# The arctangent's table booked by itself, and a one-column Gelu before the gate's tanh, in an S4D and channel-MLP kernel

## The chip, the cores and the metric

The kernel runs on one core of one Trainium2 chip. The metric is the device time of one execution in microseconds (us); the times before are three runs of the same program. The five engines have queues of their own, which run in order: TensorE (PE, with its weight loads as PEld), VectorE (DVE), ScalarE (ACT), GpSimd (POOL) and SyncE (SP, which only issues DMAs here).

## What is computed

One sequence of L = 2048 tokens with D = 576 channels goes through two branches, whose product is added to the input:

```python
x  = A_u
xn = _layernorm(x)
s  = _A_ref(xn, ...)          # S4D: a kernel K of L taps per channel, then a causal convolution by FFT
g  = _silu(_B_ref(xn, ...))   # layernorm, 576 -> 4608, tanh-Gelu, 4608 -> 576
return x + s * g
```

In `_A_ref` the taps come from 128 complex poles for each channel, `K = 2 Re sum_n C exp(A dt l)`. Everything is float32.

## The kernel before

**The MLP sets the frame.** Weights and activations are split into a high and a low float32r part, so each product is three matmuls. The 4608 hidden columns are taken in 12 groups of 384 (`G = 3` blocks of 128), the tokens in two halves of 1024, and each half in two blocks of 512: 48 slots in all, `NSLOT`. A slot has 11 positions on PE. The first three are `layer1` (L508, 14 matmuls of 512 columns each): a PSUM bank is filled, ScalarE applies Gelu (L541) and copies the high part (L544), VectorE forms the low part `hl` (L547). Gelu writes into a tile `h32` of which there are two, and which comes free when `hl` has been formed. The other eight positions are `layer2` (L565, matmuls of 288 columns), whose sums VectorE adds to `acc` (L573). Each group's weights are split on ScalarE (L488) and VectorE (L485).

**S4D fills the gaps.** `params()` turns the pole parameters into polar form once, on 128 x 576 tiles. Its ScalarE steps are Exp, Square, Sqrt, then Arctan (L709), Abs (L710) and Sin (L711, L714). The powers (Exp, L741) are made in eight packs of two halves each; `columns` (L744 to L746) puts phases and weights into a pack, which L753 sends to DRAM. From there 36 blocks of tables are built, each with two Sin on ScalarE (L802, L804) between Copy, Abs and VectorE's products; TensorE makes the taps from them (L867, copied out in L872), VectorE's `skip` (L951) adds the skip weight to the first tap, and the FFT work of a chunk of 96 channels takes the taps in (L939, L977, L1030, L1057).

**The gate.** When a half's last group has been added to `acc`, in the middle of the kernel, `gate_store` forms SiLU of the first half's sums as `z (1 + tanh(z/2))`: two halves of each of 8 tiles, so 16 Tanh of 288 columns (L578, `tanh_half`), each followed by a product on VectorE (L589). Tanh's results go into the same two `h32` tiles as Gelu's. At the same place the transposed second half of the tokens is loaded, transposed on VectorE (L1234) and split (L1239, L1241 on ScalarE, L1246, L1248 on VectorE).

**The order is planned while the program is traced.** The class `Order` keeps a clock for each engine, `od.t`, advances it by booked durations (`act(n) = 0.06 + 0.00098 n` us on ScalarE, for instance), and pins every engine's instructions in the order in which it picked them. It also keeps `od.tbl`, the function table that it thinks ScalarE holds. A step names its table in `tbl` ("gelu", "exp", "sqrt", "sin", "silu"); a step without one leaves the table as it is. A step of another table is booked 1.28 us later (`take`, L87 to L94):

```python
if tbl and tbl != self.tbl:
    free += 1.28
    self.tbl = tbl
```

A step that can wait is admitted only if it ends before the next deadline on its engine, with the load for it and the load back to Gelu counted (`advance`, L167 to L171):

```python
after = st["tbl"] or self.tbl
d += 1.28 * ((after != self.tbl) + (after not in ("gelu", "silu")))
if b > horizon or b + d > soon.get(e, 1e9) + st["late"]:
    continue
```

`soon` holds the latest start of the next Gelu. Among steps that could start, the earliest goes first, and at equal times the line that stands earlier in the list of lines: the weight split before the powers. The planner only orders: the loads themselves are put in by the compiler, in front of an activation whose function is not in the table loaded last. Instructions added inside a step's function, without a step of their own, are not booked.

Of the kernel before, what the change touches and what calls it, by code (L numbers as in the profile page):

```python
# [12 lines left out]
AF = mybir.ActivationFunctionType  # L13
# [29 lines left out]
def dve(n):  # L43
    return 0.075 + 0.00104 * n


def act(n):
    return 0.06 + 0.00098 * n
# [159 lines left out]
def step(eng, dur, fn, need=(), mark=None, cv=0, at=0.0, late=0.0, tbl=None, by=1e9):  # L208
    return dict(eng=eng, dur=dur, fn=fn, need=tuple(need), mark=mark, cv=cv, at=at, late=late, tbl=tbl, by=by)
# [3 lines left out]
def mixer_kernel(ctx, tc, u, log_a_real, a_imag, c_real, c_imag, log_dt, d_skip, w1, b1, w2, b2,  # L213
                 f1, f2, g2, g1, tvals, ident, out, parts=("mlp", "s4d")):
    nc = tc.nc
# [40 lines left out]
    tv, small = tvs[:, :NV], tvs[:, NV:]  # L256
    b1t = sb.tile([P, F // P], F32, name="b1t")
    halfpi, epst = small[:, 0:2], small[:, 2:4]
# [316 lines left out]

    def tanh_half(z):
        t = sb.tile([P, TB], F32, name="h32", bufs=2)[:, :288]
        nc.scalar.activation(t, z, AF.Tanh, scale=0.5)  # L578
        return t

    def gate_store(j, dh):
        z = acc[:, j, dh * 288:dh * 288 + 288]
        T = []

        def one():
            T.append(tanh_half(z))

        def two():
            nc.vector.scalar_tensor_tensor(z, T[0], 1.0, z, op0=OP.add, op1=OP.mult)  # L589
            if dh:  # L590
                nc.gpsimd.dma_start(g_s[j], acc[:, j])
        return one, two
# [71 lines left out]
    def params():  # L664
# [4 lines left out]
        add = lambda *a, **k: out.append(step(*a, **k))  # L669
# [14 lines left out]
        V, A = nc.vector, nc.scalar  # L684
        e, d = act(D) + 0.1, dve(D)
# [15 lines left out]
        t = T[2]  # L701
# [4 lines left out]
            add("DVE", 1.9, lambda h=h: V.reciprocal(t[:, h], t[:, h]))  # L706
        add("DVE", d, lambda: V.scalar_tensor_tensor(ci, T[4], 1.0, ci, op0=OP.subtract, op1=OP.mult))
        add("DVE", d, lambda: V.tensor_mul(t, t, ci))
        add("ACT", e, lambda: A.activation(t, t, AF.Arctan), tbl="sin", late=0.0)  # L709
        add("ACT", e, lambda: A.activation(T[3], t, AF.Abs))  # L710
        add("ACT", e, lambda: A.activation(T[3], T[3], AF.Sin, bias=halfpi[:, 0:1], scale=-2.0), tbl="sin", late=0.0)  # L711
        turns(1, th)
# [379 lines left out]
    od = Order(tc, nc)  # L1092
# [234 lines left out]
    for x, y in zip((pl, pl2, pl3, pl4, pl5, pl6), params()):  # L1327
        x["steps"] += y
# [103 lines left out]
    for slot in range(NSLOT):  # L1432
# [4 lines left out]
        for pos in range(NPOS):  # L1437
# [21 lines left out]
            else:  # L1459
# [12 lines left out]
                if last or halves:  # L1472
                    add = cell[0]
# [76 lines left out]
```

## Time and profile before

| What | us |
|---|---|
| median of 3 runs (lowest to highest) | 1084.84 (1084.74 to 1085.39) |
| the profiled execution, its time | 1084.85 |
| the profiled execution, its span | 1083.1 |
| PE busy in the span | 1072.6 (99%) |
| DVE busy | 947.7 (88%) |
| ACT busy | 653.0 (60%) |
| POOL busy | 199.4 (18%) |
| mean granted TensorE clock | 0.998 |

The span runs from the first to the last recorded instruction; 1.75 us of the execution's time lie outside it. Times in rows of the timeline are microseconds from the span's start, then the duration, the engine, the source line, the operation, the tile written and the tiles read; a bracket at the end of a row holds the idle time of the engine before it, and what ended it. Matmuls overlap, so a TensorE row is longer than the distance to the next one.

### The profile page before, as it was taken

How to read it: one execution, taken by the hardware profiler on the slowest of the kernel's cores; microseconds unless marked ns; L12 is line 12 of the kernel's file. 1: busy time of each engine (PE TensorE's matmuls, PEld its weight loads, DVE VectorE, ACT ScalarE, POOL GpSimd, SP SyncE). 2: the span in 40 equal slices, each digit the busy share in tenths (PEclk: the TensorE clock that was granted, in tenths of full speed). 3: DMA queues.
4: the chain of work that ended last, by engine and by line, in shares of the span. 5: the costliest groups of instructions: out<-in, count | busy, mean ns of one | idle time of the engine just before them, and what ended most of it. 6: DMA issues, size and time to landing. Idle time of an engine off the chain costs nothing.

```text
span 1083.1 us, 27198 instructions
## 1 busy us (share of the span) xinstructions
PE 1072.6 (99%) x11491; PEld 933.4 (86%) x11491; DVE 947.7 (88%) x1518; ACT 653.0 (60%) x974; POOL 199.4 (18%) x281
## 2 busy tenths in 40 slices
PE   9999999999999999999999999999999999999997
PEld 7989999889888888888888888888888887888896
DVE  7797878989999999999999999999999996677367
ACT  6558569767666665767756667566665754233333
POOL 6559342110000200002000010000100022110231
PEclk9999999999999999999999999999999999999999
DMA  7746455823225222454423432142312347332344
GB/s 235 231 138 191 152 196 192 215 85 116 71 70 108 67 80 58 108 94 128 134 68 99 83 85 83 37 124 47 107 53 76 111 88 238 111 105 88 96 153 117
DMA packets 136537, 125.54 MB, mean 116 GB/s; under 512 B 88156, under 2 KB 108096, under 8 KB 135392
## 3 DMA queue, kind: packets, MB, share of 16 engines
q1 hardware_dynamic: 120624, 76.44, 26.4%
q0 software_dynamic: 15040, 46.40, 13.7%
q8 instruction: 90, 1.47, 0.6%
q10 hardware_dynamic: 752, 0.97, 0.3%
q14 instruction: 31, 0.25, 0.1%
HBM read 95.52 MB, written 34.01 MB: 120 GB/s over the span
## 4 chain that ended last, share of the span: by engine, by line
PE 87%; DVE 3%; ACT 1%; issue 1%; DMA 1%; POOL 0%; ACTq 0%; DVEq 0%; POOLq 0%
PE mxa L565 19%; PE mxb L565 19%; PE mxa L508 19%; PE mxb L508 19%; PE cv L977 3%; PE cv L867 3%; PE cv L1030 2%; PE cv L939 2%; PE cv L1057 1%; DMA xn_s<-w 0%; DVE hl L547 0%; ACT L541 0%; DVE acc L573 0%; DVE A L644 0%; ACT A L741 0%
## 5 line engine op out<-in xcount | busy, mean ns | idle before, releaser
L565 PE MATMUL mxa<-w2h,hh 128*128 128x288 f32 x573 | 171.4, 299 | 0.0
L565 PE MATMUL mxb<-w2h,hh 128*128 128x288 f32 x576 | 170.9, 297 | 0.0
L565 PE MATMUL mxb<-w2h,hl 128*128 128x288 f32 x576 | 170.1, 295 | 0.2 <-DVE hl L547 0.2
L565 PE MATMUL mxb<-w2l,hh 128*128 128x288 f32 x576 | 169.5, 294 | 0.0
L565 PE MATMUL mxa<-w2h,hl 128*128 128x288 f32 x573 | 169.1, 295 | 0.0
L565 PE MATMUL mxa<-w2l,hh 128*128 128x288 f32 x573 | 168.7, 294 | 0.0
L547 DVE TENSOR_TENSOR hl<-h,hh 128x512 fp32r<-128x512 f32 x144 | 99.4, 692 | 76.3 <-ACT hh L544 75.7
L541 ACT ACTIVATE h<-mxa,b1t 128x512 f32<-128x512 f32 x73 | 50.2, 689 | 126.5 <-PE mxa L508 121.8
L767 POOL DMA_DIRECT2D par<-par_s x36 | 27.3, 759 | 518.9 <-DVE mg L810 479.1
L565 PEld LDWEIGHTS mxa<-w2h,hh 128*128 128x128 f32 x573 | 107.6, 188 | 9.6 <-issue 6.0
L565 PEld LDWEIGHTS mxb<-w2h,hh 128*128 128x128 f32 x576 | 108.2, 188 | 4.9 <-issue 2.5
L565 PEld LDWEIGHTS mxb<-w2l,hh 128*128 128x128 f32 x576 | 108.1, 188 | 0.6
L565 PEld LDWEIGHTS mxb<-w2h,hl 128*128 128x128 f32 x576 | 108.1, 188 | 0.4 <-DVE hl L547 0.4
L565 PEld LDWEIGHTS mxa<-w2l,hh 128*128 128x128 f32 x573 | 107.6, 188 | 0.7
L565 PEld LDWEIGHTS mxa<-w2h,hl 128*128 128x128 f32 x573 | 107.5, 188 | 0.0
L541 ACT ACTIVATE h<-mxb,b1t 128x512 f32<-128x512 f32 x71 | 48.9, 689 | 75.9 <-PE mxb L508 73.7
L544 ACT ACTIVATE hh<-h 128x512 fp32r<-128x512 f32 x144 | 90.9, 632 | 4.0
L573 DVE TENSOR_TENSOR acc<-mxa,acc 128x576 f32<-128x576 f32 x88 | 65.4, 743 | 17.0 <-PE mxa L565 16.7
L508 PE MATMUL mxa<-XH,w1h 128*128 128x512 f32 x284 | 80.3, 404 | 0.0
L508 PE MATMUL mxb<-XH,w1h 128*128 128x512 f32 x280 | 77.3, 398 | 0.2 <-ACT h L541 0.2
L508 PE MATMUL mxa<-XL,w1h 128*128 128x512 f32 x284 | 76.2, 390 | 0.0
L508 PE MATMUL mxa<-XH,w1l 128*128 128x512 f32 x284 | 76.0, 389 | 0.0
(230 smaller groups left out, 2422.3 us busy)
## 6 DMA issues: line engine op xcount, KB each, us to landing
raw<-in_B_w_dram SPq DMA_DIRECT2D x72, 288.0 KB, 3.5
raw<-in_B_w_dram SPq DMA_DIRECT2D x96, 192.0 KB, 3.0
par_s<-A POOLq DMA_DIRECT2D x8, 1080.0 KB, 5.9
par<-par_s POOLq DMA_DIRECT2D x36, 240.0 KB, 3.4
f2t<-f2q SPq DMA_DIRECT2D x24, 256.0 KB, 3.7
raw<-in_B_w_dram SPq DMA_DIRECT2D x48, 96.0 KB, 3.5
u_s<-in_A_u_dram POOLq DMA_DIRECT2D x16, 288.0 KB, 4.4
xc<-xn_s SPq DMA_DIRECT2D x48, 96.0 KB, 3.9
```

What stands on the lines that cost most here:

```text
L508: nc.tensor.matmul(q, a, b, start=j == 0, stop=j == len(ops) - 1)
L541: nc.scalar.activation(t, q, AF.Gelu_apprx_tanh, bias=b1t[:, g * G + i:g * G + i + 1], scale=1.0)
L544: LAST[0] = nc.scalar.activation(hh[:, i], t, AF.Copy)
L547: nc.vector.tensor_sub(hl[:, i], t, hh[:, i].bitcast(F32))
L565: nc.tensor.matmul(q[:, dh, :288], a[:, i, c], b[:, i, d], start=i == 0 and k == 0, stop=i == G - 1 and k == 2)
L573: nc.vector.tensor_add(o, q[:, dh:dh + n, :288], b if g == 0 else o)
L767: nc.gpsimd.dma_start(PAR[b].rearrange("p (g i) k -> p g (i k)", g=4), dram(par_s, (b // 6 * CH + b % 6 * 4) * NPAR, [[D * NPAR, P], [24 * ...
L867: nc.tensor.matmul(q[32 * g:32 * g + 32, i // 2, i % 2 * 64:i % 2 * 64 + 64], U[:, ri, 4 * g + i, :], v[:, ri, 4 * g + i, :], start=ri == ...
L939: nc.tensor.matmul(Q1ST[i, x][g // 2][64 * f:64 * f + 64, g % 2].rearrange(order), f1t[r].rearrange("p s k -> p (s k)"), rhs(r, f), start= ...
L977: nc.tensor.matmul(Q[i][32 * q:32 * q + 32, f, 2 * ri:2 * ri + 2], m[r, 4 * i + q, 32 * ri:32 * ri + 32], A2[r, 4 * p + 2 * i + q // 2, :, ...
L1030: nc.tensor.matmul(QI[q // 2][64 * f:64 * f + 64, q % 2, i], MAT["g2t", p + i // 2][r, i % 2, ri], YS[p + i // 2][0][r, i % 2, ri, f], sta ...
L1057: nc.tensor.matmul(Q[f][32 * e:32 * e + 32, t], g1t[r], A2[r, k:k + 2, 1].rearrange("p i d r -> p i r d"), start=True, stop=True, skip_gro ...
```

## The change

Two edits. The step of the arctangent names a table of its own, "arctan", where it had named "sin". And `tanh_half` applies Gelu to one column, into a spare column of the tile of small constants, in front of Tanh, when the planner's `od.tbl` is not "gelu" at that moment; the planner books nothing for it, and nothing reads the column. What is computed is the same.

```diff
     def tanh_half(z):
         t = sb.tile([P, TB], F32, name="h32", bufs=2)[:, :288]
+        if od.tbl != "gelu":
+            nc.scalar.activation(small[:, 5:6], epst[:, 0:1], AF.Gelu_apprx_tanh)
         nc.scalar.activation(t, z, AF.Tanh, scale=0.5)
         return t
...
-        add("ACT", e, lambda: A.activation(t, t, AF.Arctan), tbl="sin", late=0.0)
+        add("ACT", e, lambda: A.activation(t, t, AF.Arctan), tbl="arctan", late=0.0)
         add("ACT", e, lambda: A.activation(T[3], t, AF.Abs))
         add("ACT", e, lambda: A.activation(T[3], T[3], AF.Sin, bias=halfpi[:, 0:1], scale=-2.0), tbl="sin", late=0.0)
```

## The prediction

> **What bounds the kernel now.** I read the page first: the busy shares, then the engines of the chain that ended last.
>
> ```profile
> PE 1072.6 (99%) x11491; PEld 933.4 (86%) x11491; DVE 947.7 (88%) x1518; ACT 653.0 (60%) x974; POOL 199.4 (18%) x281
> PE 87%; DVE 3%; ACT 1%; issue 1%; DMA 1%; POOL 0%; ACTq 0%; DVEq 0%; POOLq 0%
> ```
>
> TensorE is busy all but 10.5 us of a span of 1083.1, and the chain runs along it. The change touches ScalarE alone, which is busy 60%. So what it can bring is what TensorE still waits for on ScalarE, directly or through VectorE. The view of TensorE's waits, asked for 90 to 1058 us, names all of that:
>
> ```profile
> PE cv L939 <- DVE kt L951: 0.4, 1, 0.4
> PE mxb L508 <- ACT h L541: 0.2, 1, 0.2
> PE mxb L565 <- DVE hl L547: 0.2, 1, 0.2
> ```
>
> Three waits in 970 us. These are idle times after the modelled end of the matmul before; what a wait costs is the distance from one start to the next, less the usual distance. The timeline of TensorE around the three:
>
> ```profile
> 97.25 1.07 PE L508 MATMUL mxa<-XH,w1l 128*128 128x512 f32 x4
> ...
> 98.39 0.39 PE L508 MATMUL mxa<-XR,w1s 128*128 128x512 f32 x1
> 99.00 1.21 PE L508 MATMUL mxb<-XH,w1h 128*128 128x512 f32 x4 [0.23 <-ACT h L541]
> ...
> 522.43 0.30 PE L565 MATMUL mxb<-w2h,hh 128*128 128x288 f32 x1
> 522.56 0.29 PE L565 MATMUL mxb<-w2l,hh 128*128 128x288 f32 x1
> 523.04 0.40 PE L565 MATMUL mxb<-w2h,hl 128*128 128x288 f32 x1 [0.19 <-DVE hl L547]
> ...
> 543.06 0.29 PE L565 MATMUL mxb<-w2h,hl 128*128 128x288 f32 x1
> 543.75 0.58 PE L939 MATMUL cv<-kt,f1t 32*64 32x384 f32 x8 [0.40 <-DVE kt L951]
> ```
>
> Four 512-column matmuls take 1.07, the last of them 0.39, so their usual distance is (1.07 - 0.39) / 3 = 0.23; for 288 columns it is 522.56 - 522.43 = 0.13. The first wait then costs 99.00 - 98.39 - 0.23 = 0.38, and the four matmuls behind it take 1.21 in place of 1.07, another 0.14: **0.52 us**. The second costs 523.04 - 522.56 - 0.13 = 0.35, and 0.40 in place of 0.29 behind it: **0.46**. The third costs 543.75 - 543.06 - 0.13 = **0.56**. Together 1.54 us. That is the most that a ScalarE edit can take out of this part of the kernel, and all three waits lie where the two edits act: the first right behind the polar form's arctangent and sine, the other two in the stretch of the gate's tanh.
>
> **Part 1, the booking of the arctangent.** ScalarE's timeline there:
>
> ```profile
> 86.18 1.28 ACT L709 ACT_TABLE_LOAD   x1
> ...
> 88.90 1.28 ACT L711 ACT_TABLE_LOAD   x1
> ...
> 91.00 1.28 ACT L741 ACT_TABLE_LOAD   x1
> 92.29 2.00 ACT L741 ACTIVATE A<-A 128x1008 f32<-128x1008 f32 x2
> 94.19 1.81 ACT L488 ACTIVATE w2h<-raw 128x576 fp32r<-128x576 f32 x3
> 95.91 1.04 ACT L741 ACTIVATE A<-A 128x1008 f32<-128x1008 f32 x1
> 96.97 1.28 ACT L541 ACT_TABLE_LOAD   x1
> 98.26 0.69 ACT L541 ACTIVATE h<-mxb,b1t 128x512 f32<-128x512 f32 x1
> ...
> 107.21 1.05 ACT L741 ACTIVATE A<-A 128x1008 f32<-128x1008 f32 x1
> ...
> 115.26 0.69 ACT L541 ACTIVATE h<-mxa,b1t 128x512 f32<-128x512 f32 x1 [5.70 <-PE mxa L508]
> ```
>
> The chip loads a table for the arctangent and another for the sine. The planner, for which both are "sin", books one. So it thinks that ScalarE is free 1.28 us sooner than it is, admits three exponentials behind the sine, and the Gelu that frees TensorE's bank starts at 98.26, late: TensorE's first wait. No load disappears on the chip by this edit. What it does is an order. With both loads booked, ScalarE's clock in the plan stands 1.28 later behind the sine, and the last exponential, which must end with its way back to Gelu (1.2 + 1.28 in the code) before the Gelu's latest start, no longer fits. Worked through from the code's durations, which decide the order and give no time here, it would start on the plan's clock at 94.65 and be back at Gelu at 94.65 + 1.20 + 1.28 = 97.13, for a latest start of 97.24; 1.28 later it doesn't fit. By the rule of equal times the three weight splits now go ahead of the second exponential, which still just fits; if it doesn't, it is deferred with the other, and the Gelu starts sooner still. Without the 1.04 at 95.91 the Gelu can start at 98.26 - 1.04 = 97.22 and end at 97.91, before TensorE asks for the bank at 98.39 + 0.23 = 98.62. The first wait goes: -0.52.
>
> What is late next is the deferred exponential. It finds its place at 107.21, behind the other one, where the table is already loaded and ScalarE then stands idle for 5.70 us before 115.26; 1.05 us fit five times. Its reader is `columns`, which comes much later, because it also needs the end of VectorE's polar arithmetic:
>
> ```profile
> 118.47 0.45 DVE L746 TENSOR_TENSOR A<-A,xc 128x288 f32<-128x288 f32 x1
> ...
> 120.64 0.45 DVE L746 TENSOR_TENSOR A<-A,xc 128x288 f32<-128x288 f32 x1
> ```
>
> The pack in question is the second, at 120.64; the exponential would be ready at about 109.3. So nothing else moves, the planner's clocks and table are the same again when the Gelu of 115.26 is due, and from there it should write the order of before. The cost of the deferral is nothing, under the cover of that idle time; were the cover gone, it would be one more pair of loads, 2.57 us of ScalarE, in the next gap. No DMA is issued by the moved step, and it passes none.
>
> **Part 2, the Gelu before the tanh.** The rows of the group of table loads, of the price of a one-column activation (L1165 is one, of the same form), and the two places:
>
> ```profile
> L578 ACT ACT_TABLE_LOAD x2 | 2.6, 1283 | 0.0
> L1165 ACT ACTIVATE tv<-tv 128x1 f32<-128x1 f32 x1 | 0.2, 203 | 0.0
> ```
>
> ```profile
> 509.46 1.28 ACT L578 ACT_TABLE_LOAD   x1
> 510.75 0.78 ACT L578 ACTIVATE h<-acc 128x288 f32<-128x288 f32 x2
> ...
> 512.82 1.28 ACT L541 ACT_TABLE_LOAD   x1
> 514.11 0.69 ACT L541 ACTIVATE h<-mxa,b1t 128x512 f32<-128x512 f32 x1
> 514.70 0.43 ACT L578 ACTIVATE h<-acc 128x288 f32<-128x288 f32 x1
> ...
> 520.98 0.64 ACT L544 ACTIVATE hh<-h 128x512 fp32r<-128x512 f32 x1
> ...
> 530.53 1.28 ACT L578 ACT_TABLE_LOAD   x1
> ...
> 533.83 1.28 ACT L541 ACT_TABLE_LOAD   x1
> 535.13 0.69 ACT L541 ACTIVATE h<-mxb,b1t 128x512 f32<-128x512 f32 x1
> ```
>
> ```profile
> 515.16 0.46 DVE L589 SCALAR_TENSOR_TENSOR acc<-h,acc 128x288 f32<-128x288 f32 x1 [1.25 <-ACT h L578]
> ...
> 522.30 0.68 DVE L547 TENSOR_TENSOR hl<-h,hh 128x512 fp32r<-128x512 f32 x1
> ...
> 536.18 0.46 DVE L589 SCALAR_TENSOR_TENSOR acc<-h,acc 128x288 f32<-128x288 f32 x1 [1.20 <-ACT h L578]
> ```
>
> Twice a tanh stands behind a sine, and twice it is loaded with a table that has no Gelu, so that the next Gelu loads again, at 512.82 and 533.83. Gelu's table does hold tanh: the tanh at 514.70 runs behind a Gelu without a load, and so do 14 of the 16. With a Gelu in front, the load at 509.46 becomes Gelu's, the tanh behind it needs none, and the loads at 512.82 and 533.83 go. Each place saves 1.28 - 0.20 = 1.08 us of ScalarE; the dummy itself waits for nothing new, since its input was written at the start and its column is ScalarE's own. The first tanh comes up to 0.2 later, which VectorE would feel only if it stood idle for it; in the first place its idle time is elsewhere.
>
> What of this reaches TensorE goes through VectorE. It stands idle 1.25 before 515.16 and 1.20 before 536.18, each time for the tanh that sits behind the second load and a Gelu. 1.08 sooner there, VectorE has the rest of its queue 1.08 sooner, as far as its other inputs allow. For `hl` at 522.30 that is the high part, which ends at 520.98 + 0.64 = 521.62: `hl` can come 0.68 sooner, and TensorE needs 0.35. The second wait goes: -0.46. For the third, VectorE's queue from 536.18 on is full up to L951, which ended just before 543.75; 0.56 sooner is wanted, 1.08 on offer, and ScalarE, whose own queue is what feeds that stretch, moves by the same. Its Gelu at 535.13 must not run into TensorE, whose bank is long full there. The third wait goes: -0.56. It is the least sure, since four engines meet there.
>
> **The sum.** -0.52 - 0.46 - 0.56 = -1.54 against the profiled execution's 1084.85: 1083.31, say **1083.3**. That execution stands 0.01 from the median of the runs, 1084.84, so nothing is added. At the floor only the first wait goes (1084.3). A change of under 0.2%, 2.2 us, is about what a measurement of this kernel can tell from none; the forecast lies under that, at 0.14%.
>
> **The rivals.**
>
> *The waits come back.* TensorE runs ahead by 1.54 us and meets the next late input, VectorE's above all, which is the second busiest engine. Against it: the three waits are the only ones in 970 us, so margins elsewhere are mostly ample. Between two thirds and none of the gain stay: 1083.8 to 1084.85. Chance 0.13.
>
> *The back end already puts Gelu's table in.* The Trainium skill, ScalarE activation tables: per-element evaluation and per-set limits, section Table sets in the compiler and the runtime, has the back end place loads by the greedy longest run. By that rule a tanh followed by Gelus would get the table that holds both, and a Gelu in front could not remove a load. Here the trace disagrees: the tanh's own load at 509.46 is followed by the Gelu's at 512.82, with only tanh and a copy between. As a mechanism of this kernel, without any word of a page: if the loads were not saved, part 2 would add 2 x 0.20 us on ScalarE and part 1 alone would count, 1084.85 - 0.52 = 1084.3. Chance 0.02.
>
> *The plan doesn't come back to itself* (slower). If ScalarE's clock or table in the plan still differs at 115.26, every later pick can differ, and the whole S4D part is written in another order up to 1014 us. An order drawn anew has waits of its own, at about 0.5 each by the three above. Before had three; with eight or more, 5 x 0.5 = 2.5 us are added: 1087.4. It decides where the deferred exponential lands: behind 107.21 all is as before, behind 115.26 not. The 5.70 us of idle time speak against it. Chance 0.14 that the order differs; 0.08 that it is slower by over 0.2%, 0.06 that it lies within.
>
> *More than the three waits.* Faster by over 2.2 us needs 0.6 us more than TensorE's waits hold; it could come only from the start or from the tail behind the last matmul, or from small delays that the view of waits doesn't list. Chance 0.09, at 1082.5.
>
> **How the numbers follow.** Forecast 0.62, waits come back 0.13, no load saved 0.02, another order without a measurable cost 0.06: these lie within 0.2%, 0.83 in sum. Another order that costs more, 0.08, is slower; more than the three waits, 0.09, is faster. The range takes in the forecast, the return of the waits up to no change with the spread of the runs (1085.4), and 0.6 us below the forecast: 1082.7 to 1085.4.
>
> **What would show each step.** Right: two loads fewer at L541, the two of the tanh line now before one-column activations of 203 ns; between 91.0 and 98 one exponential less, the Gelu there at about 97.2, two exponentials in a row at 107.2; TensorE without the waits at 99.0, 523.0 and 543.8; the order of every engine behind 115 us as before, shifted. Wrong: loads still at 512.8 and 533.8, powers behind 115.3, or TensorE's waits on VectorE above 0.8 us in sum.

## The result and the profile after

The median went from 1084.66 us (22 runs, 1084.06 to 1085.39) to 1082.93 (22 runs, 1082.51 to 1083.95). The ratio is 0.9986, with a 95% interval of 0.9979 to 0.9992: faster by 1.5 us, within 0.9 to 2.3. The profiled execution took 1082.74, against 1084.85, and its span is 1081.0 against 1083.1.

First the page of the changed kernel, busy shares and the engines of the chain that ended last:

```profile
PE 1071.7 (99%) x11491; PEld 933.9 (86%) x11491; DVE 947.9 (88%) x1518; ACT 650.7 (60%) x974; POOL 199.1 (18%) x281
PE 98%; DVE 1%; issue 1%; DMA 0%; ACT 0%; POOL 0%; ACTq 0%; POOLq 0%; DVEq 0%
```

ScalarE has the same number of instructions, two loads less and two one-column activations more, and its busy time fell by 2.3. The chain now stays on TensorE for 98% of the span, where it was 87%: it no longer leaves TensorE in the middle. The view of TensorE's waits, 90 to 1058 us, has its two heading lines and no row:

```profile
core 0 of [0], span 1081.0 us
engine line waited for: us in total, times, longest us
```

ScalarE's timeline of the changed kernel, at the polar form and at the two places of the gate (from line 579 on, the source lines are two higher than before):

```profile
90.82 1.28 ACT L743 ACT_TABLE_LOAD   x1
92.11 1.06 ACT L743 ACTIVATE A<-A 128x1008 f32<-128x1008 f32 x1
93.07 1.81 ACT L488 ACTIVATE w2h<-raw 128x576 fp32r<-128x576 f32 x3
94.79 1.04 ACT L743 ACTIVATE A<-A 128x1008 f32<-128x1008 f32 x1
95.84 1.28 ACT L541 ACT_TABLE_LOAD   x1
97.14 0.69 ACT L541 ACTIVATE h<-mxb,b1t 128x512 f32<-128x512 f32 x1
...
106.46 1.99 ACT L743 ACTIVATE A<-A 128x1008 f32<-128x1008 f32 x2
...
114.52 0.69 ACT L541 ACTIVATE h<-mxa,b1t 128x512 f32<-128x512 f32 x1 [4.76 <-PE mxa L508]
...
508.51 1.28 ACT L579 ACT_TABLE_LOAD   x1
509.80 0.20 ACT L579 ACTIVATE tv<-tv 128x1 f32<-128x1 f32 x1
509.91 0.76 ACT L580 ACTIVATE h<-acc 128x288 f32<-128x288 f32 x2
...
511.92 0.69 ACT L541 ACTIVATE h<-mxa,b1t 128x512 f32<-128x512 f32 x1
...
530.22 0.20 ACT L579 ACTIVATE tv<-tv 128x1 f32<-128x1 f32 x1
...
532.24 0.67 ACT L541 ACTIVATE h<-mxb,b1t 128x512 f32<-128x512 f32 x1
```

One exponential is left behind the splits, the Gelu starts at 97.14, the deferred one runs with its neighbour at 106.46, and 4.76 us of idle time are left behind them. At the gate the load belongs to the one-column Gelu, and the Gelus of 511.92 and 532.24 come without one.

TensorE at the places of the three waits, its timeline in the changed kernel:

```profile
98.20 0.39 PE L508 MATMUL mxa<-XR,w1s 128*128 128x512 f32 x1
98.43 1.07 PE L508 MATMUL mxb<-XH,w1h 128*128 128x512 f32 x4
...
521.62 0.29 PE L565 MATMUL mxb<-w2l,hh 128*128 128x288 f32 x1
521.75 0.29 PE L565 MATMUL mxb<-w2h,hl 128*128 128x288 f32 x1
...
541.66 0.29 PE L565 MATMUL mxb<-w2h,hl 128*128 128x288 f32 x1
541.88 0.89 PE L941 MATMUL cv<-kt,f1t 32*64 32x384 f32 x15
```

All three are gone, and so is the longer run of matmuls behind the first: 1.07 for four, where it had been 1.21 in the kernel before. Set side by side start by start, the records of TensorE, VectorE, POOL and SP stand in the same order in both profiles. ScalarE's differ in the moved exponential, two neighbours exchanged at 98.6 (a Gelu and a copy), and the table loads.

### The profile page after: what moved, and what is told of

Its sections match the earlier page's. It is cut to its first block, busy times and chain, and to the rows that moved or that the text cites. A ratio compares the mean times of both kernels' runs of the same rounds, so it can differ in the third digit from the quotient of the medians.

```text
span 1081.0 us, 27198 instructions
## 1 busy us (share of the span) xinstructions
PE 1071.7 (99%) x11491; PEld 933.9 (86%) x11491; DVE 947.9 (88%) x1518; ACT 650.7 (60%) x974; POOL 199.1 (18%) x281
## 4 chain that ended last, share of the span: by engine, by line
PE 98%; DVE 1%; issue 1%; DMA 0%; ACT 0%; POOL 0%; ACTq 0%; POOLq 0%; DVEq 0%
PE mxa L508 22%; PE mxa L565 21%; PE mxb L565 21%; PE mxb L508 21%; PE cv L869 3%; PE cv L979 3%; PE cv L1032 2%; PE cv L941 2%; PE cv L1059 1%; DMA idp<-in_ident_dram 0%; PE mxa L523 0%; PE cv L413 0%; DVE A L646 0%; DVE row L386 0%; DVE acc L573 0%
## 5 line engine op out<-in xcount | busy, mean ns | idle before, releaser
L565 PE MATMUL mxa<-w2h,hh 128*128 128x288 f32 x573 | 171.3, 299 | 0.0
L565 PE MATMUL mxb<-w2h,hh 128*128 128x288 f32 x576 | 170.9, 297 | 0.0
L565 PE MATMUL mxb<-w2h,hl 128*128 128x288 f32 x576 | 170.0, 295 | 0.0
L565 PE MATMUL mxb<-w2l,hh 128*128 128x288 f32 x576 | 169.6, 294 | 0.0
L565 PE MATMUL mxa<-w2h,hl 128*128 128x288 f32 x573 | 169.1, 295 | 0.0
L565 PE MATMUL mxa<-w2l,hh 128*128 128x288 f32 x573 | 168.7, 294 | 0.0
L565 PEld LDWEIGHTS mxa<-w2h,hh 128*128 128x128 f32 x573 | 107.6, 188 | 9.4 <-issue 6.3
L565 PEld LDWEIGHTS mxb<-w2h,hh 128*128 128x128 f32 x576 | 108.2, 188 | 4.9 <-issue 2.5
L565 PEld LDWEIGHTS mxb<-w2l,hh 128*128 128x128 f32 x576 | 108.1, 188 | 0.6
L565 PEld LDWEIGHTS mxa<-w2l,hh 128*128 128x128 f32 x573 | 107.6, 188 | 0.7
L565 PEld LDWEIGHTS mxb<-w2h,hl 128*128 128x128 f32 x576 | 108.1, 188 | 0.0
L565 PEld LDWEIGHTS mxa<-w2h,hl 128*128 128x128 f32 x573 | 107.5, 188 | 0.0
L508 PE MATMUL mxa<-XH,w1h 128*128 128x512 f32 x284 | 80.2, 404 | 0.0
L508 PE MATMUL mxb<-XH,w1h 128*128 128x512 f32 x280 | 77.1, 397 | 0.0
L508 PE MATMUL mxa<-XL,w1h 128*128 128x512 f32 x284 | 76.2, 390 | 0.0
L508 PE MATMUL mxa<-XH,w1l 128*128 128x512 f32 x284 | 76.0, 389 | 0.0
```

The costliest lines, as they stand in the source:

```text
L508: nc.tensor.matmul(q, a, b, start=j == 0, stop=j == len(ops) - 1)
L565: nc.tensor.matmul(q[:, dh, :288], a[:, i, c], b[:, i, d], start=i == 0 and k == 0, stop=i == G - 1 and k == 2)
```

## The experiments

Each matmul starts at some time in the kernel under test and at some time in the kernel before; the difference of the two (this kernel's start less before's) is the shift. Below, a step is the change of the shift at a wait: -0.36 means that the wait is 0.36 us shorter than before.

**One edit alone.** First the arctangent's booking:

```diff
 # against the kernel before
-A.activation(t, t, AF.Arctan), tbl="sin", late=0.0
+A.activation(t, t, AF.Arctan), tbl="arctan", late=0.0
```

> Only the arctangent's booking, without the Gelu in front of tanh. Theory (each edit takes away the waits next to it): TensorE's wait at 99.0 goes, the waits near 523 and 543.8 stay with 0.46 and 0.56 and the small one near 547.2 (0.24, which VectorE's addition to acc ends) too; 0.5 to 0.6 us less than before, about 1084.1. Rival (the gain comes from a stretch that runs ahead, so that one edit alone brings most of it): the waits near 523 and 543 shrink too, 1083.2 or less. Rival (the waits in the middle are fixed by the sequence of all engines and grow to take back what was gained earlier): no change, 1084.66.

Measured: 1084.15, ratio 0.9996 (0.9987 to 1.0005). The interval holds no change; the trace is what decides. TensorE's waits in it:

```profile
PE cv L939 <- DVE kt L951: 0.4, 1, 0.4
PE mxb L565 <- DVE hl L547: 0.2, 1, 0.2
```

The wait of L508 is gone, the two others stand as they were. The shift steps by -0.36 at 99.0 and by -0.16 over the matmuls behind it, -0.52 in sum, and by nothing at 523, 543.8 and 547.2 (a fourth wait, which is shown further below). Then the other edit:

```diff
 # against the kernel before
+        if od.tbl != "gelu":
+            nc.scalar.activation(small[:, 5:6], epst[:, 0:1], AF.Gelu_apprx_tanh)
         nc.scalar.activation(t, z, AF.Tanh, scale=0.5)
```

> Only the Gelu in front of tanh; the arctangent is booked as a sine's table as before. Theory: the wait at 99.0 stays (0.5), those near 523, 543.8 and 547.2 go; 0.46 + 0.56 + 0.24 = 1.26 less than before, about 1083.4. Rival (gain mostly from running ahead of the first wait): under 0.6 less. Both edits' gains add up to that of the change if the theory holds.

Measured: 1083.49, ratio 0.9990 (0.9982 to 0.9999). Its waits:

```profile
PE mxb L508 <- ACT h L541: 0.2, 1, 0.2
```

Steps of -0.46 at 523.0, -0.48 at 543.8 and -0.24 at 547.2: 1.18 in sum. The two edits add, 0.52 + 1.18 = 1.70, and neither needs the other.

**The order, or the booking.** The step of the exponential before the deferred one does both, so that the program is the change's but for that one instruction:

```diff
 # against the changed kernel
+                fn, deps = (lambda p=p: powers(p)), [("scaled", i, p)]
+                if (i, p) == (0, 1):
+                    fn, deps = (lambda: (powers(1), carried[0](0))), [("scaled", 0, 1), ("scaled", 1, 0)]
+                elif (i, p) == (1, 0):
+                    carried.append(powers)
+                    fn = lambda: None
-                power.append(step("ACT", 1.2, lambda p=p: powers(p), tbl="exp", late=0.0, need=[("scaled", i, p)]))
+                power.append(step("ACT", 1.2, fn, tbl="exp", late=0.0, need=deps))
```

> The change with the one exponential that it deferred put back ahead of the Gelu: the step of the exponential before it does both, without a booking of its own, so that the planner's clocks and the order of all else are the change's. Theory (the order is the gain of the first edit, the number of table loads is not): the Gelu there starts at about 98.2 again and TensorE's wait of about 0.5 at 99.0 is back, the waits in the middle stay away; 0.5 to 0.6 more than the change, about 1083.5. Rival (the deferral is not what removed the wait): the wait stays away, 1082.9.

Measured: 1083.16, ratio 0.9988 (0.9979 to 0.9998). The median stands 0.23 above the change's where 0.5 was expected; the two come from different rounds, and these medians can't tell 0.2 from 0.5. TensorE's timeline has the wait back:

```profile
98.31 0.39 PE L508 MATMUL mxa<-XR,w1s 128*128 128x512 f32 x1
98.89 1.20 PE L508 MATMUL mxb<-XH,w1h 128*128 128x512 f32 x4 [0.19 <-ACT h L541]
```

0.58 - 0.23 = 0.35 and 0.13 in the four matmuls behind it; at 523, 543.8 and 547.2 the steps are those of the tanh's edit alone. What the first edit brings is one instruction's place.

**The load, or the instruction.** The same one-column activation with Tanh as its function:

```diff
 # against the kernel with the tanh's edit alone
-            nc.scalar.activation(small[:, 5:6], epst[:, 0:1], AF.Gelu_apprx_tanh)
+            nc.scalar.activation(small[:, 5:6], epst[:, 0:1], AF.Tanh)
```

> In the place of the one-column Gelu a one-column Tanh, the arctangent booked as before; so the instruction is there, but the table that is loaded has no Gelu. Theory (what counts is that a load less is made): the loads in front of the next Gelu near 512.8 and 533.8 stay, all four waits of TensorE stay, about 0.1 to 0.2 of ScalarE's time is added at two places; 1084.7 to 1085.0. Rival (an instruction that waits for nothing lets the table be loaded earlier, and this is the gain): the waits near 523 and 543.8 shrink by 0.2 or more, 1084.2 or less.

Measured: 1084.84, ratio 1.0005 (0.9996 to 1.0014), and all waits of before. ScalarE's timeline:

```profile
510.40 1.28 ACT L579 ACT_TABLE_LOAD   x1
511.69 0.20 ACT L579 ACTIVATE tv<-tv 128x1 f32<-128x1 f32 x1
...
513.77 1.28 ACT L541 ACT_TABLE_LOAD   x1
```

The extra instruction by itself brings nothing: the second load is made again at 513.77, and the times can't be told from those of before.

**Each place alone.** The condition is narrowed by the planner's clock, in the kernel with the tanh's edit alone:

```diff
-        if od.tbl != "gelu":
+        if od.tbl != "gelu" and od.t["ACT"] < 520.0:     # first place; > 520.0: second place
```

> Gelu in front of tanh only at the first of the two places (near 509), the arctangent booked as before. Theory (each load saved serves the wait that follows it): waits of TensorE at 99.0 (0.5), near 543.8 (0.56) and 547.2 (0.24) stay, the one near 523 goes; 0.46 less than before, about 1084.2. Rival (the first saving carries through to the later waits): those near 543.8 and 547.2 shrink too.

> Gelu in front of tanh only at the second place (near 530.5). Theory: the waits at 99.0 and near 523 stay, those near 543.8 and 547.2 go; 0.8 less than before, about 1083.9. Rival: the wait near 543.8 needs both savings and stays in part.

Measured, one time each beside 1084.94 of before: 1083.88 and 1083.83. In the first, TensorE steps by -0.44 at 523.0, by -0.08 at 543.8 and by nothing at 547.2; in the second by nothing at 523.0, -0.46 at 543.8 and -0.24 at 547.2. TensorE's waits with the first place alone:

```profile
PE cv L941 <- DVE kt L953: 0.3, 1, 0.3
PE mxb L508 <- ACT h L541: 0.2, 1, 0.2
```

Each load that goes serves what follows it within 20 us; the first carries on to the third wait by no more than 0.08. The two times are lower than these steps make them (0.52 and 0.70); single executions of before lie up to 1.5 apart, so here the steps are the evidence, not the times.

**How much ScalarE time is needed.** Eight, then four one-column Gelus in a row in the place of one:

```diff
 # against the kernel with the tanh's edit alone
-            nc.scalar.activation(small[:, 5:6], epst[:, 0:1], AF.Gelu_apprx_tanh)
+            for _ in range(8):                             # in the other kernel 4
+                nc.scalar.activation(small[:, 5:6], epst[:, 0:1], AF.Gelu_apprx_tanh)
```

> Eight one-column Gelus in a row at each of the two places instead of one, the arctangent booked as before. In the trace of the change the next activation starts 0.11 after the start of a one-column Gelu, so eight take 0.88, and a place saves 1.28 - 0.88 = 0.40 instead of 1.17. Theory (the wait near 543.8 shrinks by what ScalarE saves, through VectorE): a wait of 0.1 to 0.3 is left there, the one near 523, which wanted 0.35, goes or leaves under 0.1; total 1083.6 to 1084.1. Rival (a load less is enough, whatever time ScalarE has): as with one Gelu, 1083.4.

> Four one-column Gelus at each of the two places, the arctangent booked as before. The run with eight showed that in a row each starts 0.23 after the one before it, and the tanh behind the last 0.11 after that one's start at the earliest: four take 3 x 0.23 + 0.11 = 0.80, and a place saves 1.28 - 0.80 = 0.48, where one saves 1.17 and eight cost 0.47. Theory (the wait near 543.8 follows ScalarE's saving through VectorE): from 0.56 in the kernel before it shrinks by about 0.4 to 0.5, to 0.05 to 0.2; the one near 523 (0.35) to 0.1 or less. Rival (what decides is only whether ScalarE's time before the first tanh grows): both waits stay as in the kernel before.

Measured, one time each: 1084.99 beside 1084.94 of before, and 1084.01 beside 1084.48. A first kernel for four (four_gelus) had other loops shortened too; it has no time and says nothing here. The expectation for eight was wrong in its price. ScalarE's timeline with eight:

```profile
510.51 1.84 ACT L580 ACTIVATE tv<-tv 128x1 f32<-128x1 f32 x8
512.26 0.76 ACT L581 ACTIVATE h<-acc 128x288 f32<-128x288 f32 x2
```

They hold ScalarE for 512.26 - 510.51 = 1.75, not 0.88, which is more than the load of 1.28 that they save. The third wait grew by 0.28:

```profile
PE cv L942 <- DVE kt L954: 0.7, 1, 0.7
PE mxb L508 <- ACT h L541: 0.2, 1, 0.2
```

The second is not listed, because the idle time in it is now 0.14, but it stayed; from start to start it is 522.76 - 522.33 - 0.13 = 0.30, where it had been 0.35:

```profile
522.33 0.29 PE L565 MATMUL mxb<-w2l,hh 128*128 128x288 f32 x1
522.76 0.40 PE L565 MATMUL mxb<-w2h,hl 128*128 128x288 f32 x1
```

With four, ScalarE gives 0.81 (511.08 to 511.89) and saves 0.47, and the second, third and fourth waits go as with one: steps of -0.44, -0.48 and -0.24, where the expectation left 0.05 to 0.2 of the third. So a load less is not enough, and 0.47 us less are: what the three waits need is ScalarE's time.

**Another order.** The rival that spoke against the change was an order drawn anew. Three kernels differ from the changed one in the planner alone:

```diff
 # load_115 and load_140: the planner books a load at 1.15, or 1.40, in both places
-            free += 1.28
+            free += 1.15
-                        d += 1.28 * ((after != self.tbl) + (after not in ("gelu", "silu")))
+                        d += 1.15 * ((after != self.tbl) + (after not in ("gelu", "silu")))
 # exponential_late: not before 112.0 on the planner's clock
-                power.append(step("ACT", 1.2, lambda p=p: powers(p), tbl="exp", late=0.0, need=[("scaled", i, p)]))
+                power.append(step("ACT", 1.2, lambda p=p: powers(p), tbl="exp", late=0.0, at=112.0 * (i == 1 and p == 0), need=[("scaled", i, p)]))
```

> The change with the planner booking 1.15 us for a table load in place of 1.28, which makes it pick other orders on all engines from about 60 us on: an order drawn anew. Theory of the prediction's slower rival: such an order has waits of its own, of about 0.5 each; between 2 and 8 of them, 1083.5 to 1087. Other theory (the planner's deadlines keep any order almost free of waits): within 0.6 of the change.

> The change with the planner booking 1.40 us for a table load: other orders on ScalarE and VectorE, TensorE's the same. By the rival: 1083.5 to 1086; by the other theory within 0.6 of the change, 1082.4 to 1083.5.

> The change with the deferred exponential held back further, until behind the Gelus that follow 114 us. By the rival in the prediction every later pick can differ and the order doesn't come back: new waits of about 0.5, 1083.4 to 1087. Other theory: the order comes back to itself, because TensorE's turns and the deadlines are the same and the powers are made ahead of need: ScalarE's and VectorE's order differ over some tens of us, and the time is that of the change within 0.3.

Measured against before: 1087.99, ratio 1.0029 (1.0019 to 1.0038); 1082.74, ratio 0.9984 (0.9974 to 0.9993); 1082.78, ratio 0.9985 (0.9976 to 0.9994). With 1.40 the orders of ScalarE and VectorE differ from the change's here and there up to 981 us, and POOL issues one transfer sooner; TensorE's order doesn't differ, and the view lists no wait of it. In the third, the exponentials kept their place ahead of the Gelu, so it did not do what its expectation says; what changed is the planner's clock of ScalarE. The orders of ScalarE, VectorE and POOL differ from 117 us on and are the same again behind 170.

With 1.15 all engines are in another order, and that one costs. TensorE's longest wait and, from VectorE's timeline, the row that started it and the product that ended it:

```profile
PE cv L979 <- DVE pr L1000: 2.3, 1, 2.3
```

```profile
469.06 0.71 DVE L1236 STREAM_TRANSPOSE row<-row 128x512 f32<-128x512 f32 x1 [3.50 <-DMA row<-y_s]
...
473.80 0.95 DVE L1000 TENSOR_TENSOR pr<-cv,kk 128x768 f32<-128x768 f32 x1
```

VectorE stood 3.50 us before a transpose whose block had not arrived from DRAM, and the FFT's products stood behind it. It is one wait of 2.3, which goes back to a transfer, and not eight of 0.5. It is not all: the profiled execution took 1086.52, 3.8 more than the change's, and its TensorE is idle 2.5 us longer and busy 1.2 longer (page: 1072.9 of 1084.7, against 1071.7 of 1081.0); where the 1.2 lie is open, and so is what the median of 1087.99 has beyond this execution. The ten runs of this kernel also lie 4 us apart (1085.23 to 1089.2), where those of the other kernels timed in rounds lie within 1.5, but for same_function's 2.7. That the arrival of transfers makes this spread is argued, not shown.

**The kernel before, profiled again.**

> The kernel before, unchanged, profiled once more, to see which of the differences between the two profiles belong to the kernel. Expected: the waits of TensorE at 99.0, 523.0, 543.8 and 547.2 are there again to within 0.05; the 0.17 by which the two profiles differ before 16 us, and 0.15 at 443.6, differ from one execution to the next.

Measured: 1084.78. All four waits are there within 0.05. The start differs from the first profile by +0.24, and the delay at 443.6 of the first profile is not there. So of the 2.1 us between the spans of the first two profiles, 0.18 at the start and 0.17 at 443.6 belong to the execution that was profiled, not to the kernel; the four waits make up the other 1.73 (0.57, 0.44, 0.48 and 0.24).

## Why the prediction was right

**The order.** The plan came out as worked through, down to the weight splits ahead of the second exponential and the place of the deferred one (107.2 forecast, 106.46 found). The Gelu starts at 97.14 (97.22 forecast). Behind 115 us every engine's order is that of before, but for the loads and the two one-column Gelus.

**The first wait** was priced at 0.52; arctan_alone shows 0.52, the two profiles of before and after 0.57.

**The second**, 0.46: found 0.46 in tanh_alone, 0.44 in first_place. VectorE's timeline of the changed kernel shows the way it went:

```profile
512.97 0.46 DVE L591 SCALAR_TENSOR_TENSOR acc<-h,acc 128x288 f32<-128x288 f32 x1
...
520.70 0.69 DVE L547 TENSOR_TENSOR hl<-h,hh 128x512 fp32r<-128x512 f32 x1 [0.21 <-ACT hh L544]
...
541.20 0.18 DVE L953 TENSOR_TENSOR kt<-kt,dsk 128x12 f32<-128x12 f32 x1
```

The product that had stood 1.25 for its tanh doesn't wait, and `hl` now waits for ScalarE's high part, as forecast, but early enough. On the way to the third wait, L953 ends at 541.38, half a microsecond ahead of L941 at 541.88.

**The third** was priced at 0.56 and measured 0.48. The usual distance from an L565 to the next unit was taken as 0.13, but from L565 to the FFT's first matmul it is 541.88 - 541.66 = 0.22 also where nothing waits. The prediction called this wait the least sure, and its size was the term of the sum that was off.

**A fourth wait was missed.** The prediction took the three waits of the view for all that a ScalarE edit could take out here, 1.54 at most. But there is one more, at 547.2 in the kernel before: the timeline of the weight loads has it, TensorE's own doesn't name it:

```profile
547.22 0.19 PEld L565 LDWEIGHTS mxa<-w2h,hh 128*128 128x128 f32 x1 [0.21 <-DVE acc L573]
```

```profile
546.95 0.29 PE L565 MATMUL mxb<-w2h,hl 128*128 128x288 f32 x1
547.22 0.40 PE L565 MATMUL mxa<-w2h,hh 128*128 128x288 f32 x1
```

547.22 - 546.95 - 0.13 = 0.14, and 0.10 in the matmul behind it: 0.24. A matmul's record lasts 0.29, longer than its distance of 0.13, so a wait under 0.16 lies inside the record before it, and the view of TensorE's waits shows none. The second place's load paid for this one too (second_place). The two errors, -0.08 and +0.24, are small and in part cancelled, which was luck: 1.54 forecast, 0.52 + 0.46 + 0.48 + 0.24 = 1.70 by the kernels with one edit, 1.5 by the ratio, 1.73 by the medians.

**The price of the dummy** was taken as its 0.20 of busy time. The tanh behind it starts 509.91 - 509.80 = 0.11 later, so a place saves 1.28 - 0.11 = 1.17, not 1.08.

**Which table the tanhs had** was read wrongly. 14 of the 16 do run without a load of their own, but only ten of them in Gelu's table (four before the load at 509.46, five between 514.70 and 527.69, one at 535.72); the other four run behind the two loaded ones, in the table that has no Gelu (the second of the pair at 510.75, 512.35, the second of the pair at 531.82, 532.85). That Gelu's table holds tanh rests on the ten, and the argument stands.

**The rivals.** The waits did not come back. The rule of the Trainium skill (ScalarE activation tables: per-element evaluation and per-set limits, Table sets in the compiler and the runtime) that loads go by the greedy longest run is not borne out: in same_function, as in before, tanh gets a table without Gelu although Gelus follow. The page has the run counted per block; no run here shows where a block ends. The slower rival named the wrong point of decision and the wrong price: a different clock at 115 us (exponential_late) and other orders up to 981 us (load_140) cost nothing that can be measured, and the order that did cost (load_115) had one long wait, behind a transfer.

## What to carry to other kernels

Where one engine is busy 99%, list its waits one by one, price each from start to start, and ask of a change on another engine which of them it reaches: two loads less, 2.3 us of ScalarE, became 1.18, because what TensorE's three waits there wanted was little: 0.47 saved at each place of the gate was enough. The other 0.52 came from one exponential out of the way. The planner that thought that two functions share a table misplaced work by the length of a load; the gain of mending it was in the order, not in a load saved. Tanh lies in two of the tables loaded here, and the first function behind the sine decided which came: Tanh in front brought the one without Gelu (same_function), Gelu in front the one with both (tanh_alone). Where that holds, put the function in front whose table also holds what follows.

## What was not expected of the hardware

A one-column activation costs 0.11 us of ScalarE when the next activation doesn't wait for it (the tanh behind the Gelu at 509.80), but several in a row on the same column, of which each waits for the one before by a semaphore, follow each other at 0.23 (four in 0.91, eight in 1.84, of which the last is 0.20). After three of the four waits, the next matmuls of TensorE take 0.10 to 0.16 us longer in sum (0.16 behind the first, 0.11 behind the second, 0.10 behind the fourth; nothing behind the third, in front of the FFT), so such a wait costs more than its idle time. Why is not shown.
